# Counting a longer way for loads in a planned order, and splitting a weight piece one step behind its load

## The chip, the core and the metric

The kernel runs on one core of one Trainium2 chip. The metric is the device time of one execution in microseconds. Engines are named as in the profile: PE (TensorE), DVE (VectorE), ACT (ScalarE), POOL (GpSimd), SP (SyncE, which here only issues DMAs).

## The reference, cut to what matters

Local attention over chunks of 32 tokens (4 batches, 8 heads, 768 tokens, 8 memory slots), then a first feed-forward without activation, then a second one with 8 experts whose gates are balanced over tokens and experts:

```python
x = attention(q, k, v, mem_k, mem_v)              # 3072 tokens x 512
x = (x @ w_a) * (x @ w_b) @ w_out                 # d_ff = 1536
P = balanced(exp(x @ w_gate - max))               # 8 rounds over rows and columns
out = sum(P[:, e:e+1] * (np.maximum(x @ w1[e], 0) @ w2[e]) for e in range(8))
```

## The kernel before

All operands of the large products are split into a high and a low part, and a product is three matmuls of those parts (`mm3`, L263). The program has two parts, each with a list of operations of its own.

**First part.** Attention of 64 groups (four heads of 96 tokens each) fills the token buffer `xbig`. The first feed-forward works on 4 super-blocks of 768 tokens, 6 slices of 256 hidden columns and 2 halves of 384 tokens: 48 steps of `moe_step`. A step has four first products (`product`, 12 matmuls each into `pab`), copied and multiplied on ACT and DVE (`a_copy`, `times`, `g_high`, `g_low`), and four second products (`second`, 6 matmuls each into `po`) that DVE adds up in `acc2` (L573). Each slice needs its weights in six column pieces: in the first super-block they come in double width through the two halves of `dbuf`, are converted (one copy on ACT, L216, four operations on DVE, L220 to L238), stored, and split on ACT (L252) and POOL (L256); later super-blocks load the stored ones. A group of attention has scores (L398), mask and maximum on DVE, exponentials on ACT, the division on POOL, transposes (L435), a copy (L440 or L442), value products (L448).

From step 12 on the first part also prepares weights of the second part: 36 pieces (`for v in range(NV2)`), read from `in_w_ex` into one half of `dbuf` or `pbuf` in turn (L656), combined in four sums on DVE and split by two copies on ACT (L288) and four subtractions on DVE (`weight_ops`, L272), and stored again (L658). Piece v is read in step x = 12 + 31 v // 36.

**Second part.** The gates, and the second feed-forward in seven products for eight (`SEVEN`).

**What sets the order.** Nothing is ordered by hand. `Order.add` takes an operation with its engine, a cost, a due time (in steps) and those that it waits for. `Order.emit` walks through a clock of its own: whenever an engine is free, it takes the ready operation with the earliest due time. An operation of SP ends for its followers only `LAND` microseconds after it. What comes out is one list for each engine, and on the chip every engine works its list in order and waits at each operation until what it needs is there. The clock of the planner is not kept on the chip. Both parts use `Order`, the first at L364, the second at L722.

The pieces, before:

```python
old = [*prepared.get(v - 2, merged[-ND:]), products[x * 2 * NF]]
y = add("SP", 0.5, x + 0.5, lambda ...: nc.sync.dma_start(out=blocks, in_=src), *old)
prepared[v] = weight_ops(add, w, blocks, sums, x + 1.5, y, [*old, kept.get(v - 2)], pool=False)
```

`products[x * 2 * NF]` is the first product of step x, `prepared[v - 2]` the splits of the piece that used the buffer before, `kept[v - 2]` the store of its result.

Of the kernel before, what the change touches and what calls it, by code (L numbers as in the profile page):

```python
# [47 lines left out]
class Order:  # L48
# [3 lines left out]

    NEXT = 0.13
    HOP = 0.25
    LAND = 3.0

    def __init__(self):
        self.ops = []

    def add(self, engine, cost, due, f, *after):  # L60
        self.ops.append((engine, cost, due, f, [x for x in after if x is not None]))
        return len(self.ops) - 1

    def emit(self):
        follow = [[] for _ in self.ops]
        missing = [len(op[4]) for op in self.ops]
        for x, op in enumerate(self.ops):
            for y in op[4]:
                follow[y].append(x)
        BEGIN, FREE, DONE = range(3)  # L70
        ready = {op[0]: [] for op in self.ops}
        busy = dict.fromkeys(ready, False)

        events = [(0.0, x, BEGIN) for x, m in enumerate(missing) if m == 0]
        heapq.heapify(events)
        begin = [0.0] * len(self.ops)
        left = len(self.ops)
        while events:
            now = events[0][0]
            while events and events[0][0] <= now:  # L80
                _, x, what = heapq.heappop(events)
                engine, cost, due, f, after = self.ops[x]
                if what == FREE:
                    busy[engine] = False
                elif what == BEGIN:
                    heapq.heappush(ready[engine], (due, x))
                else:
                    for y in follow[x]:
                        missing[y] -= 1
                        if not missing[y]:  # L90
                            hop = self.NEXT if self.ops[y][0] == engine else self.HOP
                            heapq.heappush(events, (now + hop, y, BEGIN))
            for engine, queue in ready.items():
                if queue and not busy[engine]:
                    _, x = heapq.heappop(queue)
                    cost, f = self.ops[x][1], self.ops[x][3]
                    busy[engine] = True
                    f()
                    left -= 1
                    heapq.heappush(events, (now + cost, x, FREE))  # L100
                    land = self.LAND if engine == "SP" else 0.0
                    heapq.heappush(events, (now + cost + land, x, DONE))
        assert left == 0

# [2 lines left out]
def tile_kernel(ctx: ExitStack, tc, qT, kw, vw, w_moe, w_gate, w_ex, out):  # L107
# [12 lines left out]
    NF = FS // P  # L120
# [38 lines left out]
    def f32(ap):  # L159
        return ap.bitcast(F32)  # L160
# [110 lines left out]
    def sub(out, a, b, op=ALU.subtract, engine=None):  # L271
        (engine or nc.vector).tensor_tensor(out=out, in0=a, in1=b, op=op)  # L272

    def weight_ops(add, w, blocks, sums, due, loaded, before=(), pool=True):


        w11, w12, w22, w21 = (blocks[:, i * Q:(i + 1) * Q] for i in range(4))
        s1, s2, s3, s4 = (sums[:, i * Q:(i + 1) * Q] for i in range(4))
        d = due
        y = add("DVE", 0.42, d, lambda: sub(s1, w22, w21, ALU.add), loaded, *before)  # L280
        y = add("DVE", 0.42, d, lambda: sub(s3, w11, w21), y)
        y = add("DVE", 0.42, d, lambda: sub(s2, s1, w11), y)
        summed = add("DVE", 0.42, d, lambda: sub(s4, w12, s2), y)
        done = []
        for cost, x, a, n, y in ((0.83, 0, blocks, 3, loaded), (1.05, 3, sums, 4, summed)):
            h, lo = w[:, x:x + n, 0, :], w[:, x:x + n, 1, :]
            a = a[:, :n * Q].rearrange("p (i n) -> p i n", i=n)
            y = add("ACT", cost, d, lambda h=h, a=a: nc.scalar.activation(out=h, in_=a, func=AF.Copy), y, *before)  # L288
            done.append(y)
            if pool:  # L290
                done.append(add("POOL", 2.4 * cost, d, lambda h=h, lo=lo, a=a: sub(lo, a, f32(h), engine=nc.gpsimd), y))
                continue
            for b in range(0, n, 2):
                c = min(b + 2, n)
                done.append(add(
                    "DVE", 0.35 * (c - b), d, lambda h=h[:, b:c], lo=lo[:, b:c], a=a[:, b:c]: sub(lo, a, f32(h)), y))
        return done
# [40 lines left out]
    with ExitStack() as pa:  # L338
# [22 lines left out]

        tiles = [(b, t) for b in range(B) for t in range(NT)]

        order = Order()  # L364
        add = order.add


# [107 lines left out]
        for x in range(2 * len(tiles)):  # L475
            i, g = divmod(x, 2)

            block, y = divmod(x, GB)
# [45 lines left out]
        products, seconds, free_pab, free_po, free_a, finished = [], [], [], [], [], {}  # L524
# [122 lines left out]
        prepared, kept = {}, {}  # L647
        NV2 = NU + EARLY1
        for v in range(NV2):
            blocks, sums = places[v % 2]  # L650
            w = xbig[:, X7 + SEG * 4 + (v % 2) * 7 * UNIT:][:, :7 * UNIT].rearrange("p (i y n) -> p i y n", i=7, y=2)
            u = v - EARLY1
            src, dst = (w_ex[v, :, :W1], wc1[v]) if u < 0 else (w_ex[u, :, W1:], wc2[u // 2][:, :, u % 2, :])
            x = NS * NK + v * (len(steps) - NS * NK - 5) // NV2
            old = [*prepared.get(v - 2, merged[-ND:]), products[x * 2 * NF]]
            y = add("SP", 0.5, x + 0.5, lambda blocks=blocks, src=src: nc.sync.dma_start(out=blocks, in_=src), *old)  # L656
            prepared[v] = weight_ops(add, w, blocks, sums, x + 1.5, y, [*old, kept.get(v - 2)], pool=False)
            kept[v] = add("SP", 0.5, x + 2.0, lambda w=w, dst=dst: nc.sync.dma_start(  # L658
                out=dst, in_=f32(w.rearrange("p i y n -> p i (y n)"))), *prepared[v])

# [58 lines left out]
    pm = py[0]  # L719
    out_v = out.rearrange("(t p) d -> p t d", p=P)  # L720

    order = Order()  # L722
    add = order.add


# [483 lines left out]
```

## Time and profile before

| | us |
|---|---|
| median of 3 runs (lowest, highest) | 2775.14 (2771.87, 2779.71) |
| the profiled execution | 2776.48 |
| its span, first to last instruction | 2774.7 |
| PE busy in it | 2663.8 (96%) |
| DVE, ACT, POOL busy | 2117.0, 1040.6, 440.1 |
| mean granted PE clock | 0.98 |

Busy time counts an engine's own instructions; time in which it waits at an instruction is idle time, and the profile names what ended it. The granted clock is the share of the full TensorE clock. All times of stretches are microseconds from the span's start.

### The profile page before, as it was taken

How to read it: one execution, taken by the hardware profiler on the slowest of the kernel's cores; microseconds unless marked ns; L12 is line 12 of the kernel's file. 1: busy time of each engine (PE TensorE's matmuls, PEld its weight loads, DVE VectorE, ACT ScalarE, POOL GpSimd, SP SyncE). 2: the span in 40 equal slices, each digit the busy share in tenths (PEclk: the TensorE clock that was granted, in tenths of full speed). 3: DMA queues.
4: the chain of work that ended last, by engine and by line, in shares of the span. 5: the costliest groups of instructions: out<-in, count | busy, mean ns of one | idle time of the engine just before them, and what ended most of it. 6: DMA issues, size and time to landing. Idle time of an engine off the chain costs nothing.

```text
span 2774.7 us, 36105 instructions
## 1 busy us (share of the span) xinstructions
PE 2663.8 (96%) x13131; PEld 2287.1 (82%) x13131; DVE 2117.0 (76%) x3123; ACT 1040.6 (38%) x1888; POOL 440.1 (16%) x274
## 2 busy tenths in 40 slices
PE   7999989889899899999999999999999999999998
PEld 6889888889899678888877888888888888888886
DVE  8995576567574788889888777777779777777776
ACT  6654553444342433333333322322223332232222
POOL 4433332324220122222230000000000000000000
PEclk8999999899999999999999999999999999999999
DMA  7664676666654456666657766666667766666663
GB/s 208 197 188 143 229 240 226 209 219 212 231 188 170 145 200 229 224 220 223 241 204 256 218 198 199 199 202 202 203 199 228 217 202 200 194 203 199 201 182 106
DMA packets 237024, 565.58 MB, mean 204 GB/s; under 512 B 38145, under 2 KB 54529, under 8 KB 232753
## 3 DMA queue, kind: packets, MB, share of 16 engines
q1 hardware_dynamic: 236848, 563.28, 63.1%
q8 instruction: 105, 1.72, 0.2%
q14 instruction: 71, 0.57, 0.1%
HBM read 423.64 MB, written 139.56 MB: 203 GB/s over the span
## 4 chain that ended last, share of the span: by engine, by line
PE 48%; DVE 2%; DMA 2%; issue 0%; ACT 0%; POOL 0%; SPq 0%; ACTq 0%; DVEq 0%
PE py L263 19%; PE pa L263 13%; PE px L263 10%; PE pr L263 5%; DMA raw_e<-in_w_ex 1%; DMA raw_e<-x 1%; DVE sums L272 1%; DVE xbig L272 0%; DVE raw_e L272 0%; PE py L1082 0%; DMA out<-ostage 0%; DVE hb L272 0%; POOL wbig L272 0%; DVE part L272 0%; ACT ostage L1092 0%
## 5 line engine op out<-in xcount | busy, mean ns | idle before, releaser
L263 PE MATMUL py<-xbig,wbig 128*128 128x512 f32 x3168 | 805.9, 391 | 15.1 <-DVE sums L272 11.2
L263 PEld LDWEIGHTS py<-xbig,wbig 128*128 128x128 f32 x3168 | 594.4, 188 | 148.8 <-DVE sums L272 19.9
L970 ACT ACTIVATE xbig<-hb 128x1024 fp32r<-128x1024 f32 x336 | 354.5, 1060 | 646.6 <-PE py L263 473.5
L263 PE MATMUL pa<-xbig,wbig 128*128 128x512 f32 x2304 | 585.7, 390 | 2.7 <-ACT part L892 2.7
L263 PEld LDWEIGHTS pa<-xbig,wbig 128*128 128x128 f32 x2304 | 432.1, 188 | 92.6 <-ACT part L892 3.1
L272 DVE TENSOR_TENSOR xbig<-hb,xbig 128x1024 fp32r<-128x1024 f32 x336 | 414.8, 1236 | 93.6 <-ACT xbig L970 93.4
L272 DVE TENSOR_TENSOR sums<-py,sums 128x512 f32<-128x512 f32 x495 | 339.5, 686 | 178.6 <-PE py L263 173.6
L263 PE MATMUL pab<-xbig,wbig 128*128 128x384 f32 x2304 | 450.8, 345 | 0.4 <-ACT a_sb L546 0.4
L263 PE MATMUL px<-xbig,wbig 128*128 128x512 f32 x1728 | 443.2, 392 | 5.7 <-DVE part L272 5.0
L263 PEld LDWEIGHTS pab<-xbig,wbig 128*128 128x128 f32 x2304 | 413.2, 194 | 1.7 <-ACT a_sb L546 0.7
L263 PEld LDWEIGHTS px<-xbig,wbig 128*128 128x128 f32 x1728 | 324.4, 189 | 78.1 <-DVE part L272 10.8
L263 PE MATMUL po<-gh,wbig 128*128 128x384 f32 x768 | 241.5, 357 | 16.4 <-DVE acc L573 13.3
L272 DVE TENSOR_TENSOR hb<-hb,hb 128x1024 f32<-128x1024 f32 x192 | 235.5, 1234 | 1.0
L272 POOL TENSOR_TENSOR wbig<-raw_e,wbig 128x768 fp32r<-128x768 f32 (+1 forms) x56 | 152.1, 2717 | 490.9 <-ACT wbig L288 470.9
L263 PE MATMUL pr<-xbig,wbig 128*128 128x512 f32 x864 | 218.5, 390 | 0.2 <-DVE xbig L272 0.2
L892 ACT ACTIVATE part<-pa 128x512 f32<-128x512 f32 x192 | 114.0, 594 | 252.2 <-PE pa L263 252.1
L906 DVE SCALAR_TENSOR_TENSOR hb<-part,pb 128x512 f32<-128x512 f32 x276 | 201.6, 733 | 2.7
L263 PEld LDWEIGHTS pr<-xbig,wbig 128*128 128x128 f32 x864 | 161.7, 188 | 34.1 <-DVE xbig L272 0.6
L263 PEld LDWEIGHTS po<-gh,wbig 128*128 128x128 f32 x768 | 147.4, 195 | 24.0 <-DVE acc L573 15.7
L256 POOL TENSOR_TENSOR wbig<-raw_e,wbig 128x512 fp32r<-128x512 f32 x96 | 138.2, 1455 | 173.2 <-ACT wbig L252 139.8
L272 DVE TENSOR_TENSOR part<-px,part 128x512 f32<-128x512 f32 x192 | 131.7, 686 | 38.7 <-PE px L263 35.5
L263 PE MATMUL po<-gl,wbig 128*128 128x384 f32 x384 | 133.5, 348 | 4.0 <-DVE gl L558 3.8
(110 smaller groups left out, 2215.0 us busy)
## 6 DMA issues: line engine op xcount, KB each, us to landing
wbig<-wc SPq DMA_DIRECT2D x336, 512.0 KB, 4.0
wbig<-wc SPq DMA_DIRECT2D x476, 256.0 KB, 3.4
wc<-xbig SPq DMA_DIRECT2D x36, 1792.0 KB, 7.6
wc<-wbig SPq DMA_DIRECT2D x28, 1792.0 KB, 6.7
dbuf<-in_w_moe SPq DMA_DIRECT2D x36, 512.0 KB, 4.4
raw_e<-w_f SPq DMA_DIRECT2D x72, 256.0 KB, 6.3
raw_e<-in_w_ex SPq DMA_DIRECT2D x28, 512.0 KB, 8.5
pb<-pT SPq DMA_DIRECT2D x24, 512.0 KB, 5.0
```

Of the source, the lines that this page charges most:

```text
L256: nc.gpsimd.tensor_tensor(out=wl, in0=raw(part), in1=f32(wh), op=ALU.subtract)
L263: nc.tensor.matmul(out=out, lhsT=a, rhs=b, start=first and i + j == 0, stop=last and i == n - 1 and j == 2, skip_group_check=skip,)
L272: (engine or nc.vector).tensor_tensor(out=out, in0=a, in1=b, op=op)
L892: "ACT", 0.6, at + 0.05, lambda: nc.scalar.activation(out=parts[j], in_=src, func=AF.Copy),
L906: y = add("DVE", 0.69, due, lambda: nc.vector.scalar_tensor_tensor(out=dst, in0=src, scalar=0.0, in1=pb[:, j * HB:(j + 1) * HB], op0=ALU.m ...
L970: "ACT", 1.05, d, lambda: nc.scalar.activation(out=h, in_=src, func=AF.Copy), *deps, *t_used.get(t_n - NTR, ()))
```

## The change

The way that an SP operation takes until its followers may be placed becomes a number of each plan: 7.0 in the first part, 3.0 as before in the second. The splits of a piece also wait for the first product of the step behind that of their load.

```diff
     NEXT = 0.13
     HOP = 0.25
-    LAND = 3.0
-
-    def __init__(self):
+
+    def __init__(self, land):
         self.ops = []
+        self.land = land
...
-                    land = self.LAND if engine == "SP" else 0.0
+                    land = self.land if engine == "SP" else 0.0
                     heapq.heappush(events, (now + cost + land, x, DONE))
...
-        order = Order()
+        order = Order(7.0)
         add = order.add
...
             y = add("SP", 0.5, x + 0.5, lambda blocks=blocks, src=src: nc.sync.dma_start(out=blocks, in_=src), *old)
-            prepared[v] = weight_ops(add, w, blocks, sums, x + 1.5, y, [*old, kept.get(v - 2)], pool=False)
+            prepared[v] = weight_ops(
+                add, w, blocks, sums, x + 1.5, y, [*old, kept.get(v - 2), products[(x + 1) * 2 * NF]], pool=False)
...
-    order = Order()
+    order = Order(3.0)
     add = order.add
```

What it does to the lists is seen at two places. The first is DVE in step 29, where the 21st piece is read into `dbuf`. `a_sb<-pab` are the two `times` of a step, `dbuf<-dbuf` the four sums of the piece, `acc` the sums of second products, `pt<-t_ps` the copy of an attention group, `s_sb` and `nm` mask and maximum of the next. Before:

```order
L549 TENSOR_TENSOR a_sb<-pab,a_sb 128x384
L272 TENSOR_TENSOR dbuf<-dbuf 128x256
L573 TENSOR_TENSOR acc_154<-po,acc_154 128x384
L442 COPY pt<-t_ps 128x384
L558 TENSOR_TENSOR gl<-a_sb,gh 128x384
L573 TENSOR_TENSOR acc_154<-po,acc_154 128x384
L272 TENSOR_TENSOR dbuf<-dbuf 128x256
L272 TENSOR_TENSOR xbig<-dbuf,xbig 128x2x256
```

The first sum of the piece stands right behind the first `times` of the step in which the piece is read, in front of an accumulation and an attention copy. Now, from the second `times` of step 29 on:

```order
L549 TENSOR_TENSOR a_sb<-pab,a_sb 128x384
L407 SCALAR_TENSOR_TENSOR s_sb<-s_ps,mask_149 96x512
L422 TENSOR_SCALAR sm<-sm 96x4
L413 TENSOR_REDUCE nm<-s_sb 96x4
L425 RECIPROCAL sm<-sm 96x4
L558 TENSOR_TENSOR gl<-a_sb,gh 128x384
L272 TENSOR_TENSOR dbuf<-dbuf 128x256 x2
L407 SCALAR_TENSOR_TENSOR s_sb<-s_ps,mask_149 96x512
L272 TENSOR_TENSOR dbuf<-dbuf 128x256
L573 TENSOR_TENSOR acc_154<-po,acc_154 128x384
L422 TENSOR_SCALAR sm<-sm 96x4
L272 TENSOR_TENSOR dbuf<-dbuf 128x256
```

The first sum has moved behind the second `times` of step 29, and two sums stand together. All 36 pieces move in this way, by half a step to one step in DVE's list.

The second place is PE in steps 10 and 11, the last of the first super-block. `pab` x12 is a first product, six `po` a second one, `s_ps`, `t_ps` and `o_ps` are scores, transposes and values of attention. Before, with step 10 beginning at the third `pab` row:

```order
L263 MATMUL pab<-xbig,wbig 128x384 x12
L435 MATMUL t_ps<-ident,s_sb 128x96 x4
L263 MATMUL pab<-xbig,wbig 128x384 x12
L448 MATMUL o_ps<-pt,abuf 64x96 x4
L263 MATMUL pab<-xbig,wbig 128x384 x12
L263 MATMUL po<-gh,wbig 128x384
L263 MATMUL po<-gl,wbig 128x384
L263 MATMUL po<-gh,wbig 128x384 x2
L263 MATMUL po<-gl,wbig 128x384
L263 MATMUL po<-gh,wbig 128x384
L263 MATMUL pab<-xbig,wbig 128x384 x12
```

Now, from behind the first product of step 10 on:

```order
L435 MATMUL t_ps<-ident,s_sb 128x96 x4
L398 MATMUL s_ps<-abuf 96x128 x4
L435 MATMUL t_ps<-ident,s_sb 128x96 x4
L398 MATMUL s_ps<-abuf 96x128 x8
L435 MATMUL t_ps<-ident,s_sb 128x96 x4
L263 MATMUL pab<-xbig,wbig 128x384 x12
L398 MATMUL s_ps<-abuf 96x128 x4
L263 MATMUL pab<-xbig,wbig 128x384 x12
L398 MATMUL s_ps<-abuf 96x128 x4
L263 MATMUL pab<-xbig,wbig 128x384 x12
L398 MATMUL s_ps<-abuf 96x128 x4
L263 MATMUL pab<-xbig,wbig 128x384 x36
```

Scores of the third super-block's attention have moved in between the products, and no second products stand there any more. When step 12 begins, 40 groups have their mask on DVE, 32 before. The list of the second part is the same on every engine.

## Rows read from the trace of the kernel before

**Rows 1.** Windows: length, busy time of each engine (instructions), PE clock, DMA share, GB/s

```profile
49.30:249.20 199.90, 190.65 (x1279) 177.65 (x1278) 170.06 (x313) 114.39 (x341) 78.17 (x62) 1.00 0.59 175
249.20:809.80 560.60, 509.68 (x3077) 488.79 (x3076) 357.81 (x709) 248.23 (x616) 178.44 (x126) 0.94 0.66 225
...
876.00:2774.70 1898.70, 1863.50 (x8192) 1526.61 (x8191) 1512.08 (x1958) 630.16 (x787) 152.15 (x56) 0.99 0.64 204
```

**Rows 2.** Waits of PE, 249.2 to 809.8: us in total, times, longest

```profile
PE o_ps L448 <- DVE pt L442: 16.4, 6, 4.1
PE po L263 <- DVE acc L573: 13.3, 8, 4.7
PE o_ps L448 <- ACT pt L440: 7.9, 4, 3.5
PE pl L583 <- DVE acc L573: 5.4, 3, 3.8
```

**Rows 3.** Waits of DVE and of ACT, the same stretch

```profile
DVE pbuf L272 <- DMA pbuf<-in_w_ex: 55.4, 14, 8.2
...
DVE dbuf L272 <- DMA dbuf<-in_w_ex: 33.5, 10, 6.8
...
ACT xbig L288 <- DMA pbuf<-in_w_ex: 67.2, 13, 10.0
ACT xbig L288 <- DMA dbuf<-in_w_ex: 61.9, 15, 7.6
```

**Rows 4.** Timeline of PE, DVE, ACT, SP, step 29: start, us, ..., [idle before]

```profile
563.08 2.33 PE L263 MATMUL pab<-xbig,wbig 128*128 128x384 f32 x12
...
577.40 0.91 PE L448 MATMUL o_ps<-pt,abuf 128*64 128x96 f32 x8 [4.09 <-DVE pt L442]
...
575.98 0.42 DVE L272 TENSOR_TENSOR dbuf<-dbuf 128x256 f32<-128x256 f32 x1 [6.79 <-DMA dbuf<-in_w_ex]
...
576.04 0.84 ACT L288 ACTIVATE xbig<-dbuf 128x768 fp32r<-128x768 f32 x1 [6.29 <-DMA dbuf<-in_w_ex]
...
569.71 0.51 SPq L656 DMA_DIRECT2D dbuf<-in_w_ex  x1
```

**Rows 5.** DMA issues, 0 to 875: KB each, median us from issue to landing

```profile
dbuf<-in_w_moe SPq DMA_DIRECT2D x36, 512.0 KB, 4.4
...
dbuf<-in_w_ex SPq DMA_DIRECT2D x18, 512.0 KB, 7.3
```

**Rows 6.** Windows of single steps: 12, 20, 43

```profile
249.20:266.80 17.60, 17.60 (x106) 17.59 (x105) 9.57 (x21) 6.40 (x11) 2.65 (x2) 0.90 0.48 165
...
397.20:414.50 17.30, 17.05 (x118) 16.03 (x117) 16.29 (x31) 10.17 (x32) 10.32 (x8) 1.00 0.85 269
...
797.30:809.80 12.50, 12.50 (x74) 12.50 (x73) 5.73 (x11) 4.39 (x8) 2.54 (x2) 1.00 0.84 294
```

**Rows 7.** Timeline of SP, DVE and PE, step 40

```profile
759.26 1.59 SPq L656 DMA_DIRECT2D pbuf<-in_w_ex  x1
...
768.70 0.42 DVE L272 TENSOR_TENSOR pbuf<-pbuf 128x256 f32<-128x256 f32 x1 [8.24 <-DMA pbuf<-in_w_ex]
...
755.80 2.25 PE L263 MATMUL pab<-xbig,wbig 128*128 128x384 f32 x12
```

**Rows 8.** Timeline of PE, one block of logits

```profile
861.80 2.99 PE L583 MATMUL pl<-gate,acc 128*128 128x8 f32 x24
```

**Rows 9.** Waits of SP's list, 249.2 to 809.8

```profile
SPq L658 <- DVE xbig L272: 177.9, 24, 13.5
```

**Rows 10.** Timeline of ACT, last x2 split for the second part

```profile
827.50 1.06 ACT L318 ACTIVATE xbig<-abuf 128x1024 fp32r<-128x1024 f32 x1 [2.45 <-DVE abuf L272]
```

**Rows 11.** Groups by line, 0 to 249.2: ... | busy us, mean ns | idle before

```profile
L256 POOL TENSOR_TENSOR wbig<-raw_e,wbig 128x512 fp32r<-128x512 f32 x30 | 40.9, 1371 | 59.0 <-ACT wbig L252 40.0 <-PE s_ps L398 13.3 <-PE po L263 3.4
...
L238 DVE SCALAR_TENSOR_TENSOR raw_e<-dbuf,raw_e 128x512 int32<-128x512 int32 x24 | 19.1, 796 | 0.2
...
L216 ACT ACTIVATE raw_e<-dbuf 128x512 f32<-128x512 f32 x24 | 16.1, 671 | 27.3 <-DMA dbuf<-in_w_moe 22.6 <-issue 2.9 <-POOL wbig L256 1.7
```

## The prediction

> **What bounds the kernel now.** I read the windows first, cut where the program changes its nature. In the stretch 249.2 to 809.8 TensorE is busy 509.68 of 560.60 us, so it stands idle 50.9 us, and its mean granted clock is 0.94; before it, from 49.3 on, it loses 9.3 of 199.9 us, and behind 876 it is busy 1863.50 of 1898.70 us [rows 1]. That stretch is steps 12 to 43 of the first feed-forward, and the only one in which second-layer and early first-layer weights (`in_w_ex`, 36 pieces) are loaded and split. Next the waits of PE there: 16.4 us in front of the value products for a copy on DVE, 13.3 us in front of `po` for an accumulation on DVE, 7.9 us for the copy on ACT, 5.4 us for an accumulation in front of the logits, 43.0 of the 50.9 [rows 2]. DVE and ACT are not full there (358 and 248 of 561 us, [rows 1]); so what did they wait for? Their own waits say it: DVE 55.4 + 33.5 = 88.9 us and ACT 67.2 + 61.9 = 129.1 us for the landing of just those pieces [rows 3]. The timeline shows one case whole: the load is issued at 569.71, DVE and ACT stand until 576, the attention copy waits its turn behind DVE's subtraction, and PE starts again at 577.40 after 4.09 us of idleness [rows 4]. An engine works its list in order: a split that stands too early in the list stops all that stands behind it. The planner put it there because it counts 3.0 us from issue to landing, where these loads take 7.3 us in the median [rows 5].
>
> **The change, part by part.** No instruction is added or removed and none gets another shape. Two things move the lists of the first part: every SP operation counts 7.0 instead of 3.0 us before its users may be placed, and the splits of a piece also wait for the first product of the next step.
>
> *Splits (36 pieces, each 2 copies on ACT and 8 operations on DVE).* The load still becomes free with the first product of its step; its users come with that of the next one. A step lasts 12.5 us bare and 17.3 with attention in it [rows 6]. Against that: the worst wait of all, where the load was issued at 759.26, 1.2 us after the product of its step ended (755.80 + 2.25), and DVE went on at 768.70 [rows 7]; from product to landing that is 10.6 us, under 12.5. In the case of [rows 4] the SP list held it back by some 4 us (product ended 565.4), landing 10.6 us after it, under 17.3. So I count nearly all of the 88.9 us on DVE and 129.1 us on ACT as gone; what is left are the few pieces whose buffer comes free late because two pieces share a step.
>
> What PE gets back, from below and above. Nothing, if other waits fill the place: 0. At most the idle time and what the clock costs: 50.9 + 0.06 x 560.6 = 33.6, together 84.5 us. Between them, a stretch without stalls built up from its parts: 32 steps at 12.5 = 400; the 32 attention groups, two to a long step, at (17.3 - 12.5)/2 = 2.4 = 77; six logits blocks at 3.0 [rows 8] = 18; sum 495, and 560.6 - 495 = 66. I take this value, since its steps are rows of the same stretch at a clock of 1.00, and hold back 18 for what doesn't go: the 8 us of smaller waits that [rows 2] leaves open, and 10, a fifth of 51, for stalls of the new lists. That is -48.
>
> [...]
>
> *The new wait on DVE and ACT.* A split now waits for a product. Behind it stand accumulations, masks and `a_sb` products. The price is at most the rest of that product, 12 matmuls, about 2.1 us, and `a_sb` must wait for this product and the next in any case. From below 0, from above 36 x 2.1 = 75 us of DVE; PE feels it only where two `po` banks are full, and DVE has 203 us idle in the stretch [rows 1]. It lies within the 10.
>
> *The stores of the split weights (36, on SP) move with the splits.* SP stood 177.9 us in front of them, the longest 13.5 [rows 9], and loads queue behind. A store's wait ends with its split; the next piece's load has its step of lead to absorb it. 0, and from above what rival B counts.
>
> *The first stretch, 0 to 249.* Here the 7.0 is further off than the 3.0 was: the double-width weights land in 4.4 us [rows 5]. The new lists put the conversion of the 36 parts of the first batch later; the last stands two steps later than before. In PE's list eight groups of scores stand earlier, and in steps 10 and 11 the products stand behind bare scores, with no second products between to cover a wait. Those scores are part of the 2.4 us that a group takes, under 10 us for the eight, and what they cost here they give back after step 12. From below, -9.3: all idle time after 49.3 gone. From above see rival D. I take +4, one wait of 1 us at each of the four slices from the third on. At the other end, the x2 splits for the second part stand about one step later; the last on ACT starts at 827.50 [rows 10] and is wanted at 876, so 12.5 us more are hidden. The lists of the second part are the same as before, word for word: 0.
>
> Sum on the profiled execution (2776.5 us, span 2774.7): 2776.5 - 48 + 4 = 2732.5. It lies 1.3 above the median of the runs shown, so 2731.
>
> **The rivals.**
> A, the forecast: 2706 to 2745, chance 0.63.
> B, half of it: the splits are on time, but PE's waits are not the loads' alone. In long steps DVE would have 16 us of work in 17.3 (16.29 busy, [rows 6]), so every small lateness on it reaches PE. Then 24 of the 48 come: 2776.5 - 24 + 4 - 1.3 = 2755. For it: the step without load waits is near full on both engines. Against it: that same step, with DVE so full, lost PE only 0.25 us. 0.20.
> C, no change: the landing is not what decides; take the stalls away and the attention chain ends last instead. 2775, give or take 8. [...] The trace speaks against it: 7.3 us in the median for these loads, issued by SP [rows 5]. 0.08.
> D, slower: the first batch becomes bound by its weights. A part has a chain of landing 4.4, the Abs copy on ACT 0.67, four DVE operations of at most 0.8, the high copy on ACT (taken as long as the Abs), the low part on POOL 1.37, together 10.3 us [rows 5, 11], two at a time. The slices after the first have 15 such pairs. If each leaves 4.6 us of its chain uncovered in front of a product, that is 69 us, and 2776.5 - 48 + 69 - 1.3 = 2796. It decides from 48 / 15 = 3.2 us a pair on. For it: the bare products of steps 10 and 11. Against it: 15 pairs at 10.3 are 155 us, less than the 190.65 us that PE's own work takes from 49.3 to 249.2 [rows 1], so PE should seldom catch up. 0.09.
>
> **How the numbers follow.** About 0.3% (8 us) is what a measurement of this kernel can tell from no change: faster is below 2767. A and B lie there: 0.83; same 0.08 is C; slower 0.09 is D. The likeliest is A, 2731. For 8 in 10 the range goes from 2706 (66 and part of the first stretch, nothing held back) to 2772, through B and into C; D is left out.
>
> **What would show it.** Right: in the profile after, the waits of DVE and ACT for `in_w_ex` in the first part fall from 89 and 129 us to under 20 each; PE's idle time in steps 12 to 43 from 51 to under 20 us, its clock there from 0.94 to 0.97 or more; the first logits leave within 5 us of where they did; the part behind 876 keeps its length. Wrong: PE waits for `wbig` before step 12 (D), or the loads' waits go and PE's idle time stays, under other names (B, C).

## The result, and the profile after

The changed kernel takes 2726.22 us (median of 4 runs, 2724.66 to 2727.21) against 2775.53 (2771.87 to 2779.71): a ratio of 0.9821, 95% interval 0.9804 to 0.9838. The profiled execution took 2724.66 us, its span 2722.9. Faster was forecast, and the 2731 lie 5 us beside it.

The windows after are cut at the same places of the program as [rows 1]: the start of step 0, of step 12, of step 44 and of the second part.

```profile
48.90:269.50 220.60, 203.70 (x1371) 191.23 (x1369) 186.71 (x351) 130.46 (x415) 86.44 (x69) 0.98 0.58 168
269.50:752.40 482.90, 472.99 (x2988) 459.10 (x2988) 373.62 (x679) 237.66 (x552) 161.55 (x120) 0.99 0.74 254
752.40:823.10 70.70, 66.85 (x382) 66.26 (x381) 36.91 (x55) 17.28 (x28) 10.11 (x7) 0.95 0.35 114
823.10:2722.90 1899.80, 1864.80 (x8202) 1527.25 (x8200) 1513.35 (x1960) 629.92 (x788) 150.75 (x56) 0.99 0.64 204
```

Steps 12 to 43 lose 77.7 us (560.60 to 482.90), steps 0 to 11 gain 20.7 (199.90 to 220.60), steps 44 to 47 with the logits behind them gain 4.5 (66.20 to 70.70), and the second part is 1.1 longer (1898.70 to 1899.80). With 0.4 less in front of step 0 that is -51.8, the difference of the two spans.

A window that grows need not be waiting. In steps 0 to 11 the busy time of PE grows by 13.05 us (190.65 to 203.70) and its instructions by 92; steps 12 to 43 have 89 fewer. Most of it is work of the attention that now stands in front of step 12, but not all: the mean clock of the stretch fell from 1.00 [rows 1] to 0.98, which makes the same work some 4 us longer (an estimate: 0.02 x 220.6). So 8 to 9 us of work have moved. Steps 12 to 43 say the same: their busy time falls by 36.7 us (509.68 to 472.99), of which 28.8 are the clock by the same estimate (33.6 us lost to it before, 4.8 after), and 8 are left. The idle time of the first stretch grows by 7.7 us (9.2 to 16.9). If the moved work is put back where it was, the stage of the change gains about 69 us, and the first stretch loses about 12, in idle time and clock.

The waits of PE in steps 12 to 43, to be read beside [rows 2]:

```profile
PE o_ps L448 <- DVE pt L442: 4.6, 5, 1.9
PE po L263 <- DVE gl L558: 1.6, 1, 1.6
PE t_ps L435 <- POOL s_sb L428: 1.4, 3, 0.7
PE po L263 <- DVE acc L573: 1.3, 1, 1.3
```

The value products waited 16.4 us for `pt` on DVE and now 4.6, `po` waited 13.3 for the accumulation and now 1.3; the two others are gone from the head of the list. The waits of DVE there no longer hold a line for `in_w_ex`, where [rows 3] had 55.4 and 33.5:

```profile
DVE a_sb L549 <- PE pab L263: 37.4, 38, 3.8
DVE acc L573 <- PE po L263: 30.9, 43, 1.8
DVE xbig L272 <- ACT xbig L288: 8.5, 7, 2.9
```

What is left first is DVE waiting for PE, the right way round where PE is the bound. The waits of ACT there:

```profile
ACT a_sb L546 <- PE pab L263: 65.2, 40, 4.5
...
ACT xbig L288 <- DVE pbuf L272: 25.9, 14, 4.4
ACT xbig L288 <- DVE dbuf L272: 24.6, 12, 4.3
```

No line names `in_w_ex` here either, but the copies of the pieces wait 50.5 us for DVE's part of the same split. In the kernel before these two lines were

```profile
ACT xbig L288 <- DVE pbuf L272: 18.1, 13, 3.5
...
ACT xbig L288 <- DVE dbuf L272: 14.0, 10, 3.0
```

32.1 us, so some 18 of the 129.1 us of [rows 3] have only got another name. PE, whose own waits on ACT are gone from the head of its list, doesn't feel it.

The same kind of piece as in [rows 4], step 29, in the timeline:

```profile
541.75 0.42 SPq L656 DMA_DIRECT2D dbuf<-in_w_ex  x1
...
559.21 2.85 DVE L272 TENSOR_TENSOR dbuf<-dbuf 128x256 f32<-128x256 f32 x2
...
560.00 0.83 ACT L288 ACTIVATE xbig<-dbuf 128x768 fp32r<-128x768 f32 x1
```

Issue at 541.75, first use at 559.21, 17.5 us later, and no wait in brackets behind either row. The landing has become shorter too, 7.3 us [rows 5] to 5.7 and 5.9:

```profile
dbuf<-in_w_ex SPq DMA_DIRECT2D x18, 512.0 KB, 5.7
pbuf<-in_w_ex SPq DMA_DIRECT2D x18, 512.0 KB, 5.9
```

The new waiting in steps 0 to 11, again in the waits of PE, first two lines of before:

```profile
PE t_ps L435 <- POOL s_sb L428: 2.3, 4, 1.1
PE s_ps L398 <- DVE s_sb L407: 0.7, 1, 0.7
```

and after:

```profile
PE s_ps L398 <- DVE s_sb L407: 6.2, 6, 2.1
PE t_ps L435 <- POOL s_sb L428: 4.9, 5, 2.9
PE po L263 <- DVE gl L558: 2.6, 1, 2.6
PE o_ps L448 <- DVE xbig L459: 1.6, 3, 0.9
PE po L263 <- POOL wbig L256: 0.8, 1, 0.8
```

Scores wait 6.2 us for the mask work of the scores in front of them, transposes 4.9 us for the division on POOL. The weights of the first batch, `wbig`, cost 0.8 us.

### The profile page after: what moved, and what is told of

Same layout as the page of the kernel before. It is cut to its first block, busy times and chain, and to the rows that moved or that the text cites. A ratio compares the mean times of both kernels' runs of the same rounds, so it can differ in the third digit from the quotient of the medians.

```text
span 2722.9 us, 36104 instructions
## 1 busy us (share of the span) xinstructions
PE 2640.1 (97%) x13131; PEld 2270.2 (83%) x13131; DVE 2145.5 (79%) x3123; ACT 1043.5 (38%) x1888; POOL 426.4 (16%) x274
## 4 chain that ended last, share of the span: by engine, by line
PE 48%; DVE 2%; DMA 2%; POOL 0%; issue 0%; ACT 0%; SPq 0%; ACTq 0%; DVEq 0%
PE py L263 19%; PE pa L263 14%; PE px L263 10%; PE pr L263 5%; DMA raw_e<-in_w_ex 1%; DVE sums L272 1%; DVE xbig L272 1%; DVE raw_e L272 0%; DMA out<-ostage 0%; DMA raw_e<-x 0%; POOL wbig L272 0%; DVE hb L272 0%; PE py L1083 0%; ACT ostage L1093 0%; DVE hb L907 0%
## 5 line engine op out<-in xcount | busy, mean ns | idle before, releaser
L272 DVE TENSOR_TENSOR xbig<-hb,xbig 128x1024 fp32r<-128x1024 f32 x336 | 417.0, 1242 | 91.2 <-ACT xbig L971 91.0
L272 DVE TENSOR_TENSOR sums<-py,sums 128x512 f32<-128x512 f32 x495 | 339.6, 686 | 178.8 <-PE py L263 173.8
L263 PE MATMUL pab<-xbig,wbig 128*128 128x384 f32 x2304 | 440.9, 340 | 0.0
L263 PEld LDWEIGHTS pab<-xbig,wbig 128*128 128x128 f32 x2304 | 405.8, 190 | 1.4
L272 DVE TENSOR_TENSOR hb<-hb,hb 128x1024 f32<-128x1024 f32 x192 | 233.3, 1223 | 1.0
L272 POOL TENSOR_TENSOR wbig<-raw_e,wbig 128x768 fp32r<-128x768 f32 (+1 forms) x56 | 150.7, 2692 | 494.4 <-ACT wbig L288 474.6
L263 PEld LDWEIGHTS pr<-xbig,wbig 128*128 128x128 f32 x864 | 161.8, 188 | 33.5
L272 DVE TENSOR_TENSOR part<-px,part 128x512 f32<-128x512 f32 x192 | 131.7, 686 | 37.3 <-PE px L263 35.7
L573 DVE TENSOR_TENSOR acc<-po,acc 128x384 f32<-128x384 f32 x160 | 88.0, 551 | 60.2 <-PE po L263 59.6
```

What stands on the lines that cost most here:

```text
L263: nc.tensor.matmul(out=out, lhsT=a, rhs=b, start=first and i + j == 0, stop=last and i == n - 1 and j == 2, skip_group_check=skip,)
L573: nc.vector.tensor_tensor(out=a, in0=r["o", d], in1=a, op=ALU.add)
```

## The experiments

There are two edits, the longer way for loads (7.0) and the step that the splits wait for. Theory L says that the lead from a piece's load to its first split is all that matters, however it is made. The rivals: P, that the place of the splits behind a product matters by itself; W, that the 7.0 on the other loads gives part of the gain. All ratios are against the kernel before in runs on the same chip; e1 to e4, e5 to e8 and e9 to e12 ran on three chips, so times of different groups are compared by their ratios. "Idle" is PE's idle time in steps 12 to 43, "waits" what DVE waited there for `in_w_ex`.

**One edit at a time.** e1 leaves the step out:

```diff
-                add, w, blocks, sums, x + 1.5, y, [*old, kept.get(v - 2), products[(x + 1) * 2 * NF]], pool=False)
+                add, w, blocks, sums, x + 1.5, y, [*old, kept.get(v - 2)], pool=False)
```

> The kernel with the longer way (7.0) alone; the splits are free with their load again, as before. Theory L (what counts is the lead of the load over its splits; the longer way of all other operations is worth nothing and costs something in the first super-block): steps 0 to 11 take 221 us as in the changed kernel (200 before), and the splits stand 7 us of plan behind the load, where half of the loads land later than that, so DVE and ACT still wait for in_w_ex for 15 to 50 us each (89 and 129 before, none in the changed kernel); steps 12 to 43 come to 495 to 520 us (561 before, 483 changed), the whole to 2735 to 2765. Theory W (the longer way of all loads is what helps, the step is a trifle): steps 12 to 43 at 480 to 490, the whole at 2720 to 2732.

Measured: 2720.7 us, ratio 0.9801 [0.9785, 0.9816]. The numbers expected of L were wrong: hardly a wait is left, 3.8 us, the idle time is 4.1 us, and steps 12 to 43 take 477.1 us. The whole lies in the range given for W; what the other loads have to do with it, e6 and e7 ask below.

```profile
DVE pbuf L272 <- DMA pbuf<-in_w_ex: 2.3, 1, 2.3
DVE dbuf L272 <- DMA dbuf<-in_w_ex: 1.5, 1, 1.5
```

e2 leaves the longer way out:

```diff
-        order = Order(7.0)
+        order = Order(3.0)
```

> The kernel with the step between load and splits alone; the way is 3.0 in both parts. Theory L: no wait of DVE or ACT for in_w_ex is left (under 5 us each), steps 0 to 11 take 200 us as before, since their order is that of before, steps 12 to 43 take 490 to 502 us (483 in the changed kernel plus the 8 groups' scores that the changed kernel does before step 12), the whole comes to 2705 to 2718, faster than the changed kernel's 2726. Theory W: the whole at 2750 or more, since raw weight loads and attention loads, planned at 3.0 and landing in 5 to 8 us, go on to stop the lists.

Measured: 2717.09 us, 0.9787 [0.9774, 0.9801]; waits 0.9. Its two windows:

```profile
47.00:247.10 200.10, 191.42 (x1279) 178.24 (x1279) 170.96 (x313) 114.88 (x341) 78.81 (x62) 1.00 0.59 175
247.10:746.20 499.10, 484.64 (x3071) 469.14 (x3070) 389.88 (x707) 249.66 (x617) 168.04 (x126) 0.98 0.72 248
```

Steps 0 to 11 are what they were, in length and in PE's instructions (1279), so the 20.7 us of the change come with the longer way. Either edit alone takes the waits away; the two don't add up, and both together are slower than the step alone.

**Lead or place?** e4 goes from the kernel before, leaves the condition of the splits as it was and loads a step earlier:

```diff
-            y = add("SP", 0.5, x + 0.5, ..., *old)
+            first = [*prepared.get(v - 2, merged[-ND:]), products[(x - 1) * 2 * NF]]
+            y = add("SP", 0.5, x - 0.5, ..., *first)
```

> The kernel before, way 3.0 throughout, with the loads of the 36 pieces let go one step earlier, and the splits left at their place. Theory L (lead): waits for in_w_ex under 10 us each on DVE and ACT, steps 12 to 43 at 490 to 505, the whole at 2705 to 2722. Rival P (it is the new place of the splits in the lists, behind a step's products, that lets PE run, not the lead): steps 12 to 43 over 530, the whole over 2745.

Measured: 2715.06 us, 0.9777 [0.9764, 0.979]; waits 0, idle 10.3, steps 12 to 43 in 496.6 us. In DVE's list the splits did not move back but a little forward: the first sum of the 21st piece stands behind 58 `times`, behind 59 before. P falls: the lead is enough, from whichever end it is made.

**The way in one stretch only.** e3 keeps the step and counts 4.4 for what is due before step 10, 7.0 behind it; e8 has 7.0 before step 10 and 3.0 behind it; e5 is e3 without the step.

```diff
-                    land = self.land if engine == "SP" else 0.0
+                    land = (self.early if self.ops[x][2] < 10.0 else self.land) if engine == "SP" else 0.0
...
-        order = Order(7.0)
+        order = Order(7.0, 4.4)
```

For e8 the last line is `Order(3.0, 7.0)`.

> The changed kernel with a way of 4.4 for operations due before step 10 (the median landing of the double-width weights) and 7.0 behind. Theory L: the first super-block's cost of the longer way goes (steps 0 to 11 at 198 to 206 us), and the rest is as in the changed kernel without the early scores (490 to 502 us for steps 12 to 43): 2705 to 2718, within 6 us of the kernel with the step alone. Theory W: the 7.0 in the later steps adds something of its own, more than 6 us better than the step alone. A third reading (the 21 us that the first super-block lost are the price of scores moved forward, not of the 7.0 there): steps 0 to 43 together no shorter than in the changed kernel, 2722 to 2730.

> The kernel with the step alone (2717), with the way of 7.0 for operations due before step 10 only. It measures the price of the longer way in the first super-block by itself. If that price is real waiting: steps 0 to 11 at 221 us, steps 12 to 43 shorter by 5 to 11 us for the scores done ahead (488 to 494), and the whole 8 to 14 us slower, 2724 to 2732. If the 21 us are only scores moved across step 12: steps 0 to 43 together as in the kernel with the step alone, 696 to 702 us, and the whole within 4 us of 2717.

> A way of 4.4 for operations due before step 10 and 7.0 behind, and no step between load and splits. Reading 1 (the longer way and the step are two means to one end, the lead of the load, and do not add; the 7.0 costs about 11 us net in the first super-block): 2705 to 2714, that is the 2721 of the longer way alone less that cost, waits of DVE for in_w_ex under 10 us. Reading 2 (the step is still needed once the scores are no longer done ahead of step 12, since those scores took load off DVE): waits for in_w_ex of 20 us or more on DVE and 2725 or more.

Measured: e3 2710.4 us, 0.9759 [0.9744, 0.9775], steps 0 to 11 in 203.8 us, idle 9.8. e8 2722.92 us, 0.9822 [0.9808, 0.9835]. e5 2719.43 us, 0.981 [0.9797, 0.9824], waits 5.5. The third reading of e3 falls; L and W are not told apart by it, since it lies 6.7 us below e2, with intervals that touch. The waits of e5 are those of reading 1, its time is in neither range. The windows of e8 differ from those of e2 by the 7.0 before step 10 alone:

```profile
48.00:269.90 221.90, 206.47 (x1377) 193.36 (x1376) 189.44 (x353) 131.12 (x416) 86.97 (x70) 0.97 0.57 168
269.90:753.60 483.70, 474.37 (x2983) 460.52 (x2982) 370.34 (x676) 236.96 (x551) 161.79 (x120) 0.98 0.73 253
```

21.8 us more before step 12, 15.4 less behind it: 6.4 us lost in the two. For the whole, e2 is 58.5 us faster than the kernel before on its chip and e8 49.0 on its own, 9.5 apart. So beside the step the 7.0 in the first stretch costs 6 to 10 us and moves the rest across the border of the windows. That is the first reading of e8, though its range for steps 12 to 43 (488 to 494) was missed; the second, at most 4 us, falls.

**The way of the pieces, or of the other loads?** e6 goes from the kernel before and gives the 36 pieces' loads alone the 7.0; e7 gives it to all loads and stores but those.

```diff
+        self.way = {}
...
+                    land = self.way.get(x, self.land) if engine == "SP" else 0.0
...
+        order = Order(3.0)
...
             y = add("SP", 0.5, x + 0.5, ..., *old)
+            order.way[y] = 7.0
```

For e7 the two numbers are exchanged.

> The kernel before with the way of 7.0 for the loads of the 36 pieces alone, 3.0 for all other operations. Theory L (the lead of these loads is the gain): steps 0 to 11 at 200 us, DVE's waits for in_w_ex under 10 us (89 before), steps 12 to 43 at 485 to 503 (561 before), the whole at 2708 to 2722. Theory W (raw weight loads, attention loads and stores matter as much): steps 12 to 43 over 515, the whole over 2735.

> The kernel before with 7.0 for every operation of SP but the loads of the 36 pieces, which stay at 3.0. Theory L: DVE still waits 60 to 100 us for in_w_ex, steps 0 to 11 take 221 us, steps 12 to 43 535 to 560, the whole 2765 to 2795: no better than before, or worse by up to 20. Theory W: half of the gain or more, 2750 or less.

Measured: e6 2705.85 us, 0.9762 [0.9749, 0.9775]; e7 2755.78 us, 0.9943 [0.9929, 0.9956]. First the waits of DVE in e6, then in e7 (L273 there is L272 elsewhere), then the second window of each:

```profile
DVE pbuf L273 <- DMA pbuf<-in_w_ex: 8.4, 4, 3.3
DVE dbuf L273 <- DMA dbuf<-in_w_ex: 2.0, 2, 1.6
```

```profile
DVE pbuf L273 <- DMA pbuf<-in_w_ex: 39.5, 10, 7.7
DVE dbuf L273 <- DMA dbuf<-in_w_ex: 35.5, 12, 7.8
```

```profile
247.40:740.70 493.30, 484.87 (x3073) 467.45 (x3072) 378.06 (x707) 250.09 (x617) 173.92 (x126) 0.99 0.74 254
```

```profile
269.00:788.50 519.50, 487.81 (x2987) 471.12 (x2987) 347.28 (x677) 235.64 (x552) 165.80 (x121) 0.96 0.70 241
```

One number for 36 loads gives the whole gain, and some 16 us more than the change (0.9821 - 0.9762 = 0.59% of 2776). Its time lies 2 us under the range of L, its waits 0.4 us over; W's numbers for it are far off. e7 keeps 75 of the 89 us of waits, yet gains 0.57%, between the two theories. Its steps 12 to 43 are 41 us shorter: PE's idle time there falls from 50.9 to 31.7, the clock rises from 0.94 to 0.96 (12.8 us, estimated as above), and some 9 us are work moved in front. So some 32 us of gain come in this stage without lead for the pieces, and steps 0 to 11, 19.6 us longer with the 9 us of moved work, take some 11 of them back. Why they come is open. L holds in so far as the lead of these loads is enough; that nothing else matters, e7 contradicts.

**How far?** e9 and e10 are e6 with other numbers for the pieces, e11 is e10 with 7.0 for the loads of the unsplit weights of the later slices too.

```diff
-            order.way[y] = 7.0
+            order.way[y] = 5.0
```

> The kernel before with a way of 5.0 for the loads of the 36 pieces alone (7.0 there gave 2706 and left 10 us of DVE's 89 us of waits). Theory L (PE's idle time follows how late the landing is after the place of the split): 2 us of plan more than before; DVE's waits for in_w_ex at 35 to 60 us, steps 12 to 43 at 515 to 540, the whole 2725 to 2750. Rival (a threshold: what counts is that a split no longer stands in front of one certain accumulation or copy): either as before within 8 us, or as with 7.0 within 8 us.

> The same with 10.0. Theory L: above the longest landings, so DVE's waits for in_w_ex under 4 us and steps 12 to 43 at 485 to 493 (493 with 7.0), the whole at 2698 to 2707. Rival (later splits and stores come to press on the next piece's buffer and on SP): no better than 7.0, 2706 to 2716.

> As the one with 10.0 for the pieces, and 7.0 also for the raw weight loads of the later super-blocks (they land in 6.7 to 7.8 us there); attention loads, stores and the double-width loads of the first super-block keep 3.0. Theory L (the pieces are all): within 4 us of the one with 10.0. Theory W (the other loads matter in these steps too): 4 to 10 us faster.

| way of the pieces | waits of DVE for `in_w_ex` | steps 12 to 43 | PE idle there | time, ratio |
|---|---|---|---|---|
| 3.0 (before) | 88.9 | 560.6 | 50.9 | 1 |
| 5.0 (e9) | 36.4 | 514.9 | 25.0 | 2733.91, 0.9845 [0.9828, 0.9863] |
| 7.0 (e6) | 10.4 | 493.3 | 8.4 | 2705.85, 0.9762 [0.9749, 0.9775] |
| 10.0 (e10) | 0.7 | 495.2 | 10.6 | 2712.14, 0.9776 [0.976, 0.9791] |

The waits fall with every step, the time until 7.0, about the median landing of before; to take the last 10 us of waits away brought PE nothing. 7.0 and 10.0 are not told apart, since the intervals overlap. Of e9 the waits and the time came as L had them, and the threshold falls; of e10 L's time did not come, and the rival's number did, though no run shows its reason. e11 took 2708.59 us, 0.9763 [0.9749, 0.9776], not to be told from e10 or e6.

**The changed kernel again**, as e12, beside e9 to e11, with nothing edited:

> The changed kernel once more, beside these on one chip: 2720 to 2728, steps 0 to 11 at 221 us and steps 12 to 43 at 483 us.

Measured: 2726.64 us, 0.9825 [0.9807, 0.9842], steps 0 to 11 in 219.4 us, steps 12 to 43 in 482.8. The interval lies wholly above those of e3 and e6, so both beat the changed kernel too.

## Why the prediction was right, and where its terms were off

**The mechanism held.** The splits stood too early in the lists of DVE and ACT because the planner counted 3.0 us for a landing of 7.3. With more lead the waits went (89 us to none on DVE), PE's idle time in the stage fell from 50.9 to 9.9 us where under 20 was foreseen, and its clock rose from 0.94 to 0.99. e1, e2, e4 and e6 make the lead in four ways and get it every time; with e9 and e10 the waits follow its size. B and C fall by this, and the sum of the second part, 0, came out within 1.1 us.

**"-48" for steps 12 to 43 was too little: about -69.** The smooth stretch of 495 us, built from single steps, was the better number; it foresaw -66. The 18 us held back for new stalls were the error: after the change 9.9 us of idleness are left, but the smooth steps that I added up had small idle moments of their own (0.25 in step 20, [rows 6]), and nothing new came beyond 5 us on one line. e2, e4, e6 and e10, which move no work over the border (1279 or 1280 instructions of PE before step 12), have this stage in 493 to 499 us, 61 to 67 less than before.

**The clock** came back nearly whole: (1 - 0.94) x 560.6 = 33.6 us lost before, an estimate as above, (1 - 0.99) x 482.9 = 4.8 after. Over these steps it stood higher where PE's idle time was less: 0.94 with 50.9 us of it, 0.96 with 31.7 in e7, 0.98 with 25.0 in e9, 0.99 with 8.4 in e6. In step 12, at 0.90 before [rows 6], it fell again in the profiled execution, and rows inside the step show where:

```profile
277.83 2.74 PE L583 MATMUL pl<-gate,acc 128*128 128x8 f32 x24
280.42 3.54 PE L263 MATMUL pab<-xbig,wbig 128*128 128x384 f32 x12
...
285.19 2.24 PE L263 MATMUL pab<-xbig,wbig 128*128 128x384 f32 x12
```

```profile
281.30:284.50 3.20, 3.20 (x12) 3.20 (x11) 0.43 (x1) 0.00 (x0) 0.00 (x0) 0.50 0.22 83
```

A block of logits, 24 matmuls of 8 columns each, stands in front; behind it the clock is at 0.50, and a product takes 3.54 us where the others take 2.24. In the kernel before, the same block (251.24 to 253.98) stands in front of the same fall: the product behind it takes 3.57 us. PE reads as busy for all 17.60 us of that step [rows 6], since the busy time counts these small matmuls as full (2.74 us of the block's 2.74). And the fall does not belong to the step. Here is step 12 in the profile of the change, then in that of e12, the same kernel once more:

```profile
269.50:285.20 15.70, 15.70 (x92) 15.70 (x92) 4.63 (x10) 4.63 (x10) 5.04 (x4) 0.89 0.67 224
268.40:282.50 14.10, 14.10 (x92) 14.10 (x91) 4.14 (x8) 4.13 (x10) 6.46 (x5) 1.00 0.80 269
```

The same 92 matmuls, with the same block of logits among them, once at 0.89 and once at 1.00, 1.6 us apart. So neither the step nor the block brings the fall every time, and what sets the clock no run shows.

**"+4" for the first stretch was too little: about +12**, 7.7 of idle time and some 4 of clock, which the term did not have. Rival D had the place right and not the cause. PE doesn't wait for weights there (0.8 us on `wbig`): bare scores wait for masks, transposes for the division. The work of the eight groups moved ahead does give back what it costs, as foreseen, and at 8 to 9 us it is under 10. The sentence that the first logits would leave within 5 us of where they did was wrong: they start at 277.8 and not at 251.2. e1 and e2 show that the longer way alone does this.

**"0" at the end of the first part was 5.6 us behind the start of step 44.** One wait stands there that was not before. In the timeline of DVE, POOL and PE:

```profile
772.90 1.22 DVE L272 TENSOR_TENSOR xbig<-abuf,xbig 128x1024 fp32r<-128x1024 f32 x1
...
774.90 3.46 DVE L272 TENSOR_TENSOR xbig<-dbuf,xbig 128x1024 fp32r<-128x1024 f32 x2
775.47 4.02 POOL L256 TENSOR_TENSOR wbig<-raw_m,wbig 128x512 fp32r<-128x512 f32 x2 [16.98 <-ACT wbig L252]
...
778.28 2.28 DVE L272 TENSOR_TENSOR xbig<-abuf,xbig 128x1024 fp32r<-128x1024 f32 x1
780.49 1.21 DVE L272 TENSOR_TENSOR abuf<-abuf,dbuf 128x1024 f32<-128x1024 f32 x1
781.62 1.01 DVE L573 TENSOR_TENSOR acc<-po,acc 128x384 f32<-128x384 f32 x2
782.22 0.44 PE L263 MATMUL po<-gh,wbig 128*128 128x384 f32 x1 [3.68 <-DVE acc L573]
```

The splits of x2, which I let move at no cost, now stand in a bunch with nothing else between them; the accumulation stands behind the bunch, and PE waits 3.68 us for it. I had looked at the cover of their last users and not at what is queued behind them. How much of the 5.6 us this wait is stays open: e3 has it as well (3.7 us), and takes 1964.5 us from step 44 to its end, against 1964.9 before and 1970.5 after. e12, the same lists as after with the same wait, takes 1967.4, so some 3 us of the 5.6 are a difference between executions.

**What I did not ask** is whether both edits were needed. I counted them as one lead and their cost as small. Alone each gives as much or more: 0.9801 and 0.9787, together 0.9821. The errors of my sum, 21 us too little gained in steps 12 to 43 and 13 to 14 too little lost around them, are of opposite sign, and that is why 2731 came so near: the place within the range is luck, the mechanism is not.

**What stays open:** where the 32 us come from that e7 gains in steps 12 to 43 without lead for the pieces. And why e3 lies below e2 and e5 above e6 (2710.4 to 2717.1 us, 2719.4 to 2705.9): the first pair says that the 7.0 on the other loads behind step 10 (with 4.4 ahead of it) helps, the second that it harms. Nor does the price of the 7.0 ahead of step 10 hold without the step: e5, without it, is no faster than e1 (0.981 and 0.9801). The differences between e2, e3, e5 and e6 are 7 to 14 us, between lists that a planner has made anew, and no run takes one position of the list by itself.

## What to carry to other kernels

Where engines work lists in order, look first at what they wait for and not at how full they are: a load counted 4 us too short (3.0 for a landing of 7.3) stopped two engines that had a third and more of their time free [rows 1], and through them the third, which was the bound. Give the longer landing to the loads that engines are seen to wait for and to no others: the weights of the later super-blocks landed in 6.7 and 7.8 us in steps 12 to 43 of the kernel before, no line of DVE or ACT waited for them there, and 7.0 for them too (e11) made no difference that could be told. The same number on every load moved work about and left some 11 us of the gain behind without the step (e1), 16 with it. And when two edits serve the same end, price each alone before both.

## What the runs showed of the hardware

A DVE subtraction of 128x1024 takes 1.22 us (772.90 above). While POOL runs subtractions of its own (775.47 to 779.49), two take 3.46 together and a third, at 778.28, takes 2.28; the next operation of this size, at 780.49, takes 1.21 again. e12 has the same: 3.45 for the two and 2.28 for the third beside POOL's 4.02, then 1.21. So some 2 us of the 3.68 for which PE waits behind them are what the three take longer (an estimate: 3.46 + 2.28 - 3 x 1.22). Why they take longer beside POOL's, the rows don't show, and no run tested it.

The landing of a 512 KB load differs with how the lists lie: 7.3 us in the median before, 5.7 and 5.9 after, 5.1 and 5.3 in e1, with the same loads:

```profile
dbuf<-in_w_ex SPq DMA_DIRECT2D x18, 512.0 KB, 5.1
pbuf<-in_w_ex SPq DMA_DIRECT2D x18, 512.0 KB, 5.3
```
